# Retention and two MLPs: outputs and partial sums get buffers of their own, and three early steps are put in another order

## The chip, the core and the metric

The kernel runs on one core of one Trainium2 chip. The metric is the device time of one execution in microseconds (us); lower is better. The engines are named as in the profile: PE multiplies matrices (PEld loads its weights), DVE works on vectors, ACT applies functions and copies, POOL is the general engine, SP issues most of the transfers. Each engine takes its instructions in the order in which they are written in the program, and an instruction waits until what it reads has been written and what it overwrites has been read. L568 is line 568 of the kernel before.

## The reference

Four sequences of 768 tokens with 8 heads of width 64 go through a retention layer, and its output, as 3072 rows of 512, through two MLPs with 2048 hidden units each:

```python
for t in range(S):
    state = gamma * state + einsum('bhd,bhe->bhde', k[:, :, t], v[:, :, t])
    y[:, :, t] = scale * einsum('bhd,bhde->bhe', q[:, :, t], state)
x = y as (batch * seq, heads * head_dim)
h = x @ moe_w_in;   x = (h * cos(h)) @ moe_w_out
h = x @ moe2_w_in;  out = where(h >= 1, h, where(h <= -1, 0, (h + 1)**2 / 4)) @ moe2_w_out
```

All arrays are float32. Weights and activations are split into a high and a low part, and a product of 128 x 128 by 128 x 512 is made of three matmuls (high by high, low by high, high by low).

## The kernel before

**Chunks and blocks.** Retention is computed by chunks of 128 tokens. Chunk n is batch n % 4 at time n // 4, so the 24 chunks make 6 blocks of 4 chunks, 512 tokens each. For a chunk the kernel makes scores (`scores`, L475 for the first two blocks), masks them on DVE (`masks`, L522, or L528 and L541 later), and multiplies with values and with the state (`attend`, L597 and L604, later L585). `kv` (L557) makes a chunk's contribution to the state; `update` takes it out of PSUM: for chunks 0 to 3 it is a copy by ACT into `state` (L568), for chunks 4 to 7 two additions of `state` on DVE (L573), into a table `w` in one of five slots `w0` to `w4`. The slot that chunk 6's update takes, `w2`, held the decay table of the queries (`qdec`, read by `decay_q`, L463, on POOL, for chunks 4 to 7) and the keys of chunk 2. `finish_high` and `finish_low` split a chunk's output into the high part (ACT, L141) and the low part (DVE, L628) of the first MLP's input. `decay_k` (L453, POOL) scales the keys.

**Steps.** The first MLP is computed in 96 steps (k, b, j): k is the half of the hidden units (0 or 1), b the block, j one of 8 groups of 128 hidden units of that half. A step's first product (`first`, L687, 12 matmuls) makes 128 hidden units for 512 tokens in one PSUM bank; the phase is then rounded (`rounded`, ACT, L727), its fraction taken (`fraction`, DVE, L732), the cosine made (`cosine`, ACT, L738), the product h cos(h) formed (`product`, DVE, L741) and split (`high_part`, ACT, L745; `low`, DVE, L752). Three steps later the second product (`second`, L779, 12 matmuls) adds it to four banks, one for each 128 outputs of the block. Block 0 runs 5 steps, then block 1 its 8, then block 0 its last 3, then blocks 2 to 5; then the other half of the hidden units for blocks 0 to 5. The scores, attention and state work of later chunks lies between the products of the first 36 steps or so. Banks 4 and 5 take turns for the first product in the first 40 steps, banks 4 to 7 after that; banks 6 and 7 are the attention's in the first part, and one tile of both is shared by the scores, the output and the state contribution of a chunk. After the 96 steps the second MLP is computed (L991, L1007 and the lines around them).

**The order inside a step.** It is written by hand. `opening` writes it for steps 0 to 2, `act` for the others: rounding of this step, product and high part of the last step, fraction, `front`, low part of the last step, two outputs (`evacuate`), `mid`, cosine, two outputs, `fill`, `conv.advance`, `end`.

**Weights.** They come as pairs of 32-bit words (`raw`, L191, SP) and are converted in parts: `one` (two DVE instructions, L205 and L208), `two` (ACT, L215), `three` (DVE, L223), `four` (POOL, L232), `five` (ACT copy to the high part, L141) and `six` (POOL low part, L144). The first ten weights, called `w`, `w1`, `x[0]` to `x[2]` (of the first product) and `y[1]` to `y[5]` (of the second product), have their parts written out in the start and in the first steps; x[2] belongs to step 4. Later weights are converted by `conv.advance`.

**Outputs and sums.** When the last step of a block and a half has made its second product, `evacuate` takes the four banks out, each into a tile "o" of the ring "r" with 5 buffers, and SP stores it (L797). Phases of the steps are tiles of the same ring. For k = 0 the outputs are partial sums and go to DRAM (`yp`, and for block 0, which has two pieces, `yq`). For k = 1 `load_part` brings the partial sums back, into the tile of the block's own input `xt[1, b]`, once its last first product is through; L790 (DVE) adds them, into a tile of the ring "r", and SP stores it to `yT`. `load_parts` and `fetch_x` bring the input of the next block into the two buffers each of "xh" and "xl".

Of the kernel before, what the change touches and what calls it, by code (L numbers as in the profile page):

```python
# [11 lines left out]
F32 = mybir.dt.float32  # L12
F32R = mybir.dt.float32r
BF16 = mybir.dt.bfloat16
I32 = mybir.dt.int32
U32 = mybir.dt.uint32
AF = mybir.ActivationFunctionType
ALU = mybir.AluOpType
# [3 lines left out]
P = 128  # L22
C = 128
TB = 512
# [16 lines left out]
def tile_retention_mlp_mlp(  # L41
# [16 lines left out]
    nc = tc.nc  # L58
    NCH = qk.shape[0]
    T, DM = out.shape  # L60
    NF = w1.shape[0]
    NH = NF // 2
    NP = DM // P
    NC = kdec.shape[1]
    NB = T // TB
    D = 64
    CB = TB // C
    NEW = 2 * CB
    LAG = 3
# [9 lines left out]
    yp_d = [dram.tile([P, NP, TB], F32, name=f"yp{j}") for j in range(NB)]  # L79
    yq_d = dram.tile([P, NP, TB], F32, name="yq")  # L80
# [22 lines left out]
    wpool = [sbuf("wpool0", 1)]  # L103
# [71 lines left out]
    class Convert:  # L175
# [14 lines left out]
            src = (w1, w2)[self.m][self.j][:, self.a * TB:(self.a + 1) * TB]  # L190
            nc.sync.dma_start(out=self.raw.rearrange("p n w -> p (n w)"), in_=src.bitcast(I32))  # L191

        def one(self):
            if self.ready:
                self.f = spare_tile("f", self.few)
                nc.sync.dma_start(out=self.f, in_=w32_d[self.m, self.j, self.a])
                return
            n = 3 - self.late
            self.s = self.stage.tile([P, TB], I32, tag="cs", name="cs", bufs=n)
            if self.store:  # L200
                self.f = self.stage.tile([P, TB], F32, tag="cf", name="cf", bufs=n)
            else:
                self.f = spare_tile("f", self.few)
            f = self.f.bitcast(I32)
            nc.vector.tensor_scalar(  # L205
                out=self.f, in0=self.raw[:, :, 1].bitcast(F32), scalar1=2.0 ** -112, scalar2=None, op0=ALU.mult
            )
            nc.vector.tensor_scalar(  # L208
                out=f, in0=f, scalar1=3, scalar2=None, op0=ALU.logical_shift_left
            )  # L210

        def two(self):
            if self.ready:
# [132 lines left out]
    class Attention:  # L346


        def __init__(self, es):
            self.ap = es.enter_context(tc.tile_pool(name="att", bufs=1, reuse_waits="tile"))  # L350
            ac = es.enter_context(tc.tile_pool(name="attc", bufs=1))
            self.kdec_sb = ac.tile([P, NC, 2 * NP], F32, name="kdec_sb")
            self.state = [ac.tile([P, NP, D], F32, name=f"state{i}") for i in range(CB)]
            self.t, self.kd, self.v, self.qd = {}, {}, {}, {}
            self.kq, self.m, self.w = {}, {}, {}
            self.sc, self.pm, self.kvs, self.y = {}, {}, {}, {}
# [308 lines left out]
    def fetch_x():  # L665
        for t, d in coming[:3]:
            nc.sync.dma_start(out=t, in_=d)
        del coming[:3]

    def load_part(b, es, eng=nc.sync):  # L670

        for t, d in zip(xt[1, b], (yp_d[b], yq_d)[:1 + (b == 0)]):
            t = t.bitcast(F32)
            for e in es:
                eng.dma_start(out=t[:, e, :], in_=d[:, e, :])
                part.setdefault((b, e), []).append(t[:, e, :])
# [13 lines left out]
            )  # L690
        hs[k, b, j] = h

    def act(k, b, j, done=(), fill=(), mid=(), end=(), front=()):


        done = iter(done)
        now = Parts(k, b, j)
        now.rounded()
        last = parts.pop() if parts else None
        if last:  # L700
            last.high()
        now.fraction()
        for f in front:
            f()
        if last:
            last.low()
        evacuate(done, 2)
        for f in mid:
            f()
        now.cosine()  # L710
        evacuate(done, 2)
        for f in fill:
            f()
        conv.advance()
        for f in end:
            f()
        parts.append(now)
# [39 lines left out]
    def second(i, between=()):  # L757
# [24 lines left out]
            )  # L782
        return [(k, b, e, to) for e in range(NP)] if last else ()

    def evacuate(done, n):
        for k, b, e, to in itertools.islice(done, n):
            a, o = acc[k, b][e], tp.tile([P, TB], F32, tag="r", name="o", bufs=5)
            add = part.pop((b, e)) if k else []
            if add:
                nc.vector.tensor_tensor(out=o, in0=a, in1=add.pop(0), op=ALU.add)  # L790
            elif e % 2 == 0:
                nc.vector.tensor_copy(out=o, in_=a)
            else:
                nc.scalar.activation(out=o, in_=a, func=AF.Copy)
            for x in add:
                nc.gpsimd.tensor_tensor(out=o, in0=o, in1=x, op=ALU.add)
            nc.sync.dma_start(out=to[:, e, :], in_=o)  # L797
# [570 lines left out]
    def run():  # L1368
        i = 0
        with ExitStack() as es:  # L1370
            att = Attention(es)
            top.append(es.enter_context(tc.tile_pool(name="ps_att", bufs=1, space=PSUM, reuse_waits="tile")))
            stage = es.enter_context(tc.tile_pool(name="stage", bufs=1, reuse_waits="tile"))

# [41 lines left out]
            def scores(n):  # L1416
                att.scores(n, at[n])
                att.masks(n)
# [18 lines left out]
            w.three()  # L1437
            w.four()
            att.finish_low(0)
            att.finish_low(1)  # L1440
            scores(3)
            att.attend(2, single(at[2][0]))
            att.finish_high(2)
            w.five()
# [1 line left out]
            att.finish_low(2)  # L1446
            att.attend(3, single(at[3][0]))
            att.decay_k(0)
            w1.one()
            att.finish_high(3)  # L1450
            att.finish_low(3)
            w1.two()
            w1.three()
            w1.four()
# [7 lines left out]
            def opening(i, n):  # L1462


                now = Parts(*steps[i])
                if i == 0:
                    x[0].three()
                    now.rounded()
                    w1.five()
                    w1.six()  # L1470
                    now.fraction()
                    att.update(0)
                    att.decay_q(CB)
                    x[0].four()
                    att.masks(CB)
                    now.cosine()
                    att.decay_k(CB)
                elif i == 1:
                    now.rounded()
                    att.update(1)  # L1480
                    x[1].two()
                    now.fraction()
                    att.update(n)
                    att.decay_q(n + 1)
                    att.decay_k(n + 1)
                    att.decay_k(2)
                    att.decay_k(3)
                    att.masks(n + 1)
                    now.cosine()
                    x[1].three()  # L1490
                    x[1].four()
                    att.finish(n, now.product)
                else:
                    y[1].three()
                    now.rounded()
                    now.fraction()
                    att.update(n)
                    att.decay_q(n + 1)
                    y[1].four()
                    att.decay_k(n + 1)  # L1500
                    att.finish_high(n)
                    now.cosine()
                    att.masks(n + 1)
                    att.finish_low(n)
                    x[2].one()
                    y[1].five()
                    y[1].six()
                    for m in (2, 3):
                        att.update(m)
                    x[2].two()  # L1510
                    x[2].three()
                    x[2].four()
                if i != 1:
                    now.product()
                now.high_part()
                now.low()
                if i == 1:
                    y[1].one()
                    y[1].two()
                elif i:  # L1520
                    att.decay_q(n + 2)
                x[i].five()
                x[i].six()
                if i == 0:
                    x[1].one()
# [21 lines left out]
            for i in range(NH * (NB - 1)):  # L1547
# [16 lines left out]
                for n in decay if i >= LAG else ():  # L1564
                    att.decay_q(n)
                    att.decay_k(n)
                mid, end, fill, between, front = [], [], [], [], []
                for n in attend:
                    by, bk = place.get(i, (7, 6))
                    yb, kb = duo(by, bk)  # L1570
                    if NEW <= n < NEW + CB:
                        between.append(lambda n=n, yb=yb: att.attend(n, yb))
                        front.append(lambda n=n: att.finish_high(n))
                        mid.append(lambda n=n: att.finish_low(n))
                        continue
                    att.attend(n, yb)
                    att.kv(n, kb)
                    mid += [lambda n=n: att.finish(n), lambda n=n: att.update(n)]
                for n in early:
                    att.scores(n, (6, 7))  # L1580
# [13 lines left out]
                else:  # L1594
                    if i - 1 in y:
# [4 lines left out]
                        else:  # L1600
                            for f in (c.one, c.two, c.three, c.four):
                                f()
                            mid += [c.five, c.six]
                    act(*steps[i], done, fill, mid, end, front)
                    if i == LAG:
                        y[5].load(stage)
                send_x()
# [2 lines left out]
                elif i >= 2 * NH and i % NH == 2:  # L1610
                    store_parts(steps[i][1])
            i += 1
            assert not todo
            conv.slots = []
            conv.late = True
# [147 lines left out]
```

## Time and profile before

| | us |
|---|---|
| median of 3 runs | 1078.02 (1076.34 to 1080.09) |
| the profiled execution, its own time | 1080.16 |
| its span, first to last instruction | 1078.4 |
| PE busy | 1065.6 (99%) |
| DVE busy | 798.6 (74%) |
| ACT busy | 603.6 (56%) |
| POOL busy | 601.9 (56%) |

All views are of the profiled execution. A busy engine is one with an instruction in work; matmuls are pipelined, so that twelve that take 390 ns each follow each other every 227 ns, and are through in 2.72 us. "Idle before" is the time that an engine stood before an instruction, and the releaser is what ended it, inferred from the events of the semaphores: where several things were waited for, the one that came last by the records is named.

### The profile page before, as it was taken

The page shows a single profiled execution, that of the slowest core. Times are in us where ns is not written, and L with a number is a line of the kernel's source. Part 1 is how long each engine was busy: PE and PEld are TensorE (multiplying, and loading weights), DVE is VectorE, ACT ScalarE, POOL GpSimd, SP SyncE. Part 2 cuts the span into 40 slices and gives each one's busy share as a digit, 9 for nine tenths or more (in the row PEclk, how much of TensorE's full clock was granted, in tenths as well). Part 3 has the DMA queues.
Part 4 walks back from the last instruction along what each step waited for, and adds up shares of the span by engine and source line. Part 5 has one row for each costly group of instructions (what it writes and reads, how often), then busy time and mean ns, then how long its engine had stood idle before and what let it go on. Part 6 is the DMA issues. An engine that isn't in the chain of part 4 may idle for free.

```text
span 1078.4 us, 17871 instructions
## 1 busy us (share of the span) xinstructions
PE 1065.6 (99%) x6295; PEld 869.9 (81%) x6296; DVE 798.6 (74%) x1094; ACT 603.6 (56%) x1076; POOL 601.9 (56%) x515
## 2 busy tenths in 40 slices
PE   8999999999999999999999999999999999999998
PEld 5787787778888888888888888888888888888887
DVE  6977778786756547777874587778888777887875
ACT  3454333333355455555555666777668686675764
POOL 3845112221235457877997367796639886364560
PEclk9999999999999999999999999999999999999999
DMA  9579379896769579999898676989689889586642
GB/s 348 180 241 306 116 245 301 271 302 204 211 182 330 186 250 307 333 321 326 290 300 290 229 251 208 321 275 379 227 247 323 316 288 395 170 268 195 200 139 92
DMA packets 140137, 279.43 MB, mean 259 GB/s; under 512 B 15504, under 2 KB 42256, under 8 KB 140048
## 3 DMA queue, kind: packets, MB, share of 16 engines
q1 hardware_dynamic: 125072, 251.02, 70.4%
q10 hardware_dynamic: 14976, 27.27, 7.2%
q8 instruction: 50, 0.82, 0.3%
q14 instruction: 39, 0.32, 0.1%
HBM read 194.60 MB, written 83.62 MB: 258 GB/s over the span
## 4 chain that ended last, share of the span: by engine, by line
PE 91%; DVE 3%; DMA 3%; POOL 2%; issue 1%; ACT 0%; SPq 0%; DVEq 0%; POOLq 0%; ACTq 0%
PE b L779 24%; PE b L687 23%; PE b L991 20%; PE y L1007 19%; PE b L585 2%; DMA raw<-in_w 1%; PE b L1123 1%; PE b L492 1%; DVE big L1068 1%; DMA yp<-o 1%; PE b L503 1%; POOL cf L232 0%; POOL wil L144 0%; POOL kq L463 0%; DMA wo<-wp 0%
## 5 line engine op out<-in xcount | busy, mean ns | idle before, releaser
L727 ACT ACTIVATE r<-b 128x512 int32<-128x512 f32 x96 | 57.0, 594 | 185.4 <-PE b L687 123.3
L732 DVE SCALAR_TENSOR_TENSOR r<-b,r 128x512 f32<-128x512 f32 x96 | 65.9, 687 | 109.5 <-ACT r L727 105.1
L232 POOL TENSOR_TENSOR cf<-cf,cs 128x512 int32<-128x512 int32 x42 | 54.1, 1289 | 137.6 <-DVE cf L223 92.6
L1060 DVE TENSOR_TENSOR xh<-y,xh 128x1024 f32<-128x1024 f32 x86 | 105.0, 1221 | 30.6 <-PE y L1007 29.0
L779 PE MATMUL b<-gh,wo 128*128 128x512 f32 x384 | 98.4, 390 | 0.0
L1179 POOL TENSOR_TENSOR ft<-r,f 128x512 f32<-128x512 f32 x23 | 29.9, 1300 | 116.9 <-PE y L1007 86.7
L687 PE MATMUL b<-xh,wi 128*128 128x512 f32 x384 | 94.8, 389 | 0.0
L991 PE MATMUL b<-wih,wi 128*128 128x512 f32 x320 | 87.2, 390 | 0.4 <-DVE b L1171 0.4
L1060 DVE TENSOR_TENSOR xl<-y,xl 128x1024 f32<-128x1024 f32 x63 | 76.6, 1216 | 13.1 <-PE y L1007 13.1
L1007 PE MATMUL y<-gh,wo 128*128 128x512 f32 x276 | 85.0, 389 | 0.0
L779 PEld LDWEIGHTS b<-gh,wo 128*128 128x128 f32 x384 | 71.7, 188 | 16.0 <-DVE o L790 0.8
L687 PEld LDWEIGHTS b<-xh,wi 128*128 128x128 f32 x384 | 72.1, 188 | 15.0
L745 ACT ACTIVATE gh<-b 128x512 fp32r<-128x512 f32 x96 | 57.1, 595 | 43.1 <-DVE b L741 43.1
L687 PE MATMUL b<-xh,wih 128*128 128x512 f32 x192 | 76.0, 401 | 3.4 <-DVE gl L752 2.7
L779 PE MATMUL b<-gh,woh 128*128 128x512 f32 x192 | 77.3, 408 | 0.0
L687 PE MATMUL b<-xh,wil 128*128 128x512 f32 x192 | 75.0, 395 | 0.0
L779 PE MATMUL b<-gh,wol 128*128 128x512 f32 x192 | 74.0, 390 | 0.0
L991 PEld LDWEIGHTS b<-wih,wi 128*128 128x128 f32 x320 | 59.8, 188 | 13.8 <-DVE b L1171 1.3
L1007 PE MATMUL y<-wi,wo 128*128 128x512 f32 x276 | 70.0, 389 | 0.0
L1007 PE MATMUL y<-wo,wo 128*128 128x512 f32 x276 | 70.0, 389 | 0.0
L738 ACT ACTIVATE r<-r 128x512 f32<-128x512 f32 x96 | 60.6, 631 | 15.5 <-DVE r L732 15.4
L752 DVE TENSOR_TENSOR gl<-b,gh 128x512 fp32r<-128x512 f32 x96 | 65.6, 684 | 4.1 <-ACT gh L745 2.1
(174 smaller groups left out, 2789.3 us busy)
## 6 DMA issues: line engine op xcount, KB each, us to landing
wi<-wp SPq DMA_DIRECT2D x66, 512.0 KB, 4.7
raw<-in_w SPq DMA_DIRECT2D x64, 512.0 KB, 6.0
wo<-wp SPq DMA_DIRECT2D x63, 512.0 KB, 5.1
wp<-whi SPq DMA_DIRECT2D x48, 256.0 KB, 4.4
wp<-s SPq DMA_DIRECT2D x32, 256.0 KB, 4.7
w<-cf ACTq DMA_DIRECT2D x26, 256.0 KB, 5.3
xTh<-xh ACTq DMA_DIRECT2D x24, 256.0 KB, 5.6
xTl<-xl ACTq DMA_DIRECT2D x24, 256.0 KB, 5.7
```

Source lines behind the costliest of these rows:

```text
L232: nc.gpsimd.tensor_tensor(out=f, in0=f, in1=self.s, op=ALU.add)
L687: nc.tensor.matmul(out=h, lhsT=w[:, c * P:(c + 1) * P], rhs=x[:, c, :], start=(i == 0), stop=(i == len(terms) - 1),)
L727: nc.scalar.activation(out=self.r.bitcast(I32), in_=self.h, func=AF.Identity, scale=INV_2PI, bias=0.25)
L732: nc.vector.scalar_tensor_tensor(out=self.r, in0=self.h, scalar=INV_2PI, in1=self.r.bitcast(I32), op0=ALU.mult, op1=ALU.subtract,)
L738: nc.scalar.activation(out=self.r, in_=self.r, func=AF.Sin, scale=TWO_PI, bias=HALF_PI)
L745: nc.scalar.activation(out=self.gh, in_=self.h, func=AF.Copy)
L752: nc.vector.tensor_tensor(out=self.gl, in0=self.h, in1=self.gh.bitcast(F32), op=ALU.subtract)
L779: nc.tensor.matmul(out=acc[k, b][e], lhsT=w[:, s], rhs=g, start=(begin and i == 0), stop=(last and i == 2),)
L991: nc.tensor.matmul(out=to, lhsT=w[:, c * P:(c + 1) * P], rhs=x, start=begin and n == 0, stop=n == len(terms) - 1, skip_group_check=not begin,)
L1007: nc.tensor.matmul(out=to[:, e, :], lhsT=w[:, e * P:(e + 1) * P], rhs=a, start=begin and m == 0, stop=m == 2, skip_group_check=not begin,)
L1060: nc.vector.tensor_tensor(out=a, in0=y, in1=a, op=ALU.add)
L1179: nc.gpsimd.tensor_tensor(out=o, in0=x, in1=z, op=ALU.subtract)
```

## The change

- **Ring of outputs.** A new function `out_tile` gives the tile of an output. While the attention runs, outputs 0 and 1 of a block go to a ring "o" of two buffers in the attention's pool, outputs 2 and 3 to the ring "r" as before. Outputs of block 4's first half go to the tiles of weights 15 that are not loaded yet, those of block 5's first half to tiles of weights that are used up.
- **Partial sums.** `load_part` takes new tiles "xh" (for block 0 also "xl") of the two buffers, in place of views of `xt[1, b]`; `evacuate` adds in place, into the partial sum's tile, for blocks 0 to 4 of the second half.
- **States.** The four tiles `state` move into the low-part tiles of the weights of j = 7.
- **Start.** `scores(3)`, with its masks, goes ahead of `finish_low(1)`; `w1.one` is cut in two with `finish_low(3)` between.
- **Step 2.** The copies of the states of chunks 2 and 3 go ahead of x[2].one, y[1].five and y[1].six. Product, high part and low part of step 2, and x[2].five and x[2].six, leave `opening`; the product, the high and the low part are then done in step 3 by `act`, as in all later steps.
- **Step 3.** A new list `pre` holds `finish_high`, `update` and `finish_low` of chunk 6, x[2].five and x[2].six. `act` runs the first ahead of the last step's product and the others behind it, ahead of the fraction.

```diff
-        def one(self):
+        def one(self, *which):
+            if which == (1,):
+                f = self.f.bitcast(I32)
+                nc.vector.tensor_scalar(
+                    out=f, in0=f, scalar1=3, scalar2=None, op0=ALU.logical_shift_left
+                )
+                return
...
-            self.state = [ac.tile([P, NP, D], F32, name=f"state{i}") for i in range(CB)]
+            at = [wpool[0].tile([P, TB], F32, tag=f"w{t}l{NH - 1}", name="state") for t in "io"]
+            at = [t[:, o:o + TB // 2] for t in at for o in (0, TB // 2)]
+            self.state = [t.rearrange("p (c e) -> p c e", c=NP) for t in at]
...
     def load_part(b, es, eng=nc.sync):
-        for t, d in zip(xt[1, b], (yp_d[b], yq_d)[:1 + (b == 0)]):
-            t = t.bitcast(F32)
+        ds = (yp_d[b], yq_d)[:1 + (b == 0)]
+        if b not in halves:
+            halves[b] = [xpool.tile([P, NP, TB], F32, tag=t, name="yp") for t, _ in zip(("xh", "xl"), ds)]
+        for t, d in zip(halves[b], ds):
...
-    def act(k, b, j, done=(), fill=(), mid=(), end=(), front=()):
+    def act(k, b, j, done=(), fill=(), mid=(), end=(), front=(), pre=()):
         done = iter(done)
         now = Parts(k, b, j)
         now.rounded()
         last = parts.pop() if parts else None
+        for f in pre[:1]:
+            f()
         if last:
             last.high()
+        for f in pre[1:]:
+            f()
         now.fraction()
...
+    own = []
+
+    def out_tile(k, b, e):
+        if own and callable(own[0]) and e < 2:
+            return own[0]("o", TB, 2)
+        if (k, b) == (0, NB - 2):
+            if e % 2 == 0:
+                nm = ("wi", "wo")[e // 2]
+                own.append(wpool[1].tile([P, 2, TB], F32, tag=f"{nm}{NF - 1}", name="o"))
+            return own[-1][:, e % 2, :] if e % 2 == 0 else own.pop()[:, 1, :]
+        if (k, b) == (0, NB - 1):
+            return wpool[0].tile([P, TB], F32, tag=f"woh{e}", name="o")
+        return tp.tile([P, TB], F32, tag="r", name="o", bufs=5)
+
     def evacuate(done, n):
         for k, b, e, to in itertools.islice(done, n):
-            a, o = acc[k, b][e], tp.tile([P, TB], F32, tag="r", name="o", bufs=5)
-            add = part.pop((b, e)) if k else []
+            a, add = acc[k, b][e], part.pop((b, e)) if k else []
+            o = add[0] if k and b < NB - 1 else out_tile(k, b, e)
...
             att = Attention(es)
+            own.append(att.ring)
...
             att.finish_low(0)
+            scores(3)
             att.finish_low(1)
-            scores(3)
...
-            w1.one()
             att.finish_high(3)
+            w1.one(0)
             att.finish_low(3)
+            w1.one(1)
...
                     att.finish_low(n)
+                    for m in (2, 3):
+                        att.update(m)
                     x[2].one()
                     y[1].five()
                     y[1].six()
-                    for m in (2, 3):
-                        att.update(m)
                     x[2].two()
                     x[2].three()
                     x[2].four()
-                if i != 1:
+                if i == 2:
+                    att.decay_q(n + 2)
+                    parts.append(now)
+                    return
+                if i == 0:
                     now.product()
...
                     att.attend(n, yb)
                     att.kv(n, kb)
+                    if i == LAG:
+                        pre = [
+                            lambda n=n: att.finish_high(n), lambda n=n: att.update(n),
+                            lambda n=n: att.finish_low(n), x[2].five, x[2].six,
+                        ]
+                        continue
                     mid += [lambda n=n: att.finish(n), lambda n=n: att.update(n)]
...
             i += 1
+            own.clear()
```

## Rows read from the trace of the kernel before

**Rows 1.** The page, first part: busy us (share of the span) x instructions.
```profile
PE 1065.6 (99%) x6295; PEld 869.9 (81%) x6296; DVE 798.6 (74%) x1094; ACT 603.6 (56%) x1076; POOL 601.9 (56%) x515
```

**Rows 2.** PE's waits: waiting line, releaser: us in total, times, longest.
```profile
PE b L687 <- DVE gl L752: 2.7, 2, 2.0
```

**Rows 3.** The chain that ended last, in order: start us, us, what.
```profile
5.03 12.82 DMA raw<-in_w
...
51.16 4.54 PE b L687 x12
...
61.20 2.72 PE b L687 x12
...
89.05 3.01 PE b L687 x12
...
216.57 3.02 PE b L687 x12
...
578.27 3.28 PE b L779 x12
```

**Rows 4.** Timeline of PE: start us, us, instruction [idle before <-releaser].
```profile
42.83 1.09 PE L597 MATMUL b<-kq,state 64*64 64x128 f32 x16 [0.80 <-POOL kd L453]
...
50.00 1.16 PE L475 MATMUL b<-qk 64*128 64x128 f32 x16 [1.64 <-issue]
```

**Rows 5.** Timeline of ACT, at three places.
```profile
40.02 0.63 ACT L738 ACTIVATE r<-r 128x512 f32<-128x512 f32 x1 [1.55 <-DVE r L732]
...
42.37 0.64 ACT L568 ACTIVATE state<-b 128x256 f32<-128x256 f32 x2
...
87.07 0.60 ACT L727 ACTIVATE r<-b 128x512 int32<-128x512 f32 x1 [3.73 <-DMA yp<-o]
...
214.60 0.60 ACT L727 ACTIVATE r<-b 128x512 int32<-128x512 f32 x1 [5.54 <-PE b L779]
```

**Rows 6.** Timeline of DVE: masks and update of step 3's surroundings, step 27's product.
```profile
41.38 0.68 DVE L522 TENSOR_TENSOR w<-b,dtab 128x512 f32<-128x512 f32 x1
...
49.05 0.85 DVE L573 TENSOR_TENSOR w<-b,state 64x256 f32<-64x256 f32 x2
...
52.27 0.68 DVE L522 TENSOR_TENSOR w<-b,dtab 128x512 f32<-128x512 f32 x1
...
211.75 0.69 DVE L741 TENSOR_TENSOR b<-b,r 128x512 f32<-128x512 f32 x1
```

**Rows 7.** Timeline of POOL around step 3.
```profile
46.62 1.29 POOL L463 TENSOR_TENSOR kq<-qk,w 128x512 f32<-128x512 f32 x1
47.87 1.29 POOL L144 TENSOR_TENSOR wil<-cf,wih 128x512 fp32r<-128x512 f32 x1
49.10 1.05 POOL L453 TENSOR_TENSOR kd<-kd,kdec_sb 128x512 f32<-128x512 f32 x1
```

**Rows 8.** Windows: us, busy us by engine (instructions), PE's granted clock, DMA share, GB/s.
```profile
48.00:50.00 2.00, 0.36 (x3) 0.04 (x1) 1.96 (x5) 1.38 (x3) 2.00 (x2) 1.00 0.02 8
...
52.00:54.00 2.00, 2.00 (x6) 1.52 (x5) 1.93 (x5) 0.91 (x2) 1.26 (x2) 0.50 0.53 143
...
215.00:220.00 5.00, 3.43 (x44) 2.66 (x48) 4.07 (x8) 2.68 (x6) 0.00 (x0) 1.00 0.94 271
```

**Rows 9.** ACT's waits from 320 to 600 us.
```profile
ACT r L727 <- DMA yT<-o: 22.3, 3, 8.8
```

**Rows 10.** Instructions of the tile o: ns min/median/max, and landing of its stores.
```profile
L790 DVE TENSOR_TENSOR o<-b,xh x24: 677/680/691, 400.5 to 622.2; 128x512 f32<-128x512 f32 x24
...
DMA to landing us min/median/max: 2.0/3.4/9.0
```

**Rows 11.** Timeline of SP's queue at the first block's end in the second half.
```profile
402.64 4.07 SPq L797 DMA_DIRECT2D yT<-o  x4
406.77 0.42 SPq L196 DMA_DIRECT2D f<-w  x1
407.28 0.41 SPq L667 DMA_DIRECT2D xh<-xTh  x1
```

**Rows 12.** DVE's waits over the whole span.
```profile
DVE qk L528 <- DMA mtab<-in_tabs: 1.9, 1, 1.9
```

More of the change, by code (lines that the diff above doesn't have):

```diff
@@ L203, in one @@
                 self.f = spare_tile("f", self.few)
-            f = self.f.bitcast(I32)
             nc.vector.tensor_scalar(
@@ L207, in one @@
             )
-            nc.vector.tensor_scalar(
-                out=f, in0=f, scalar1=3, scalar2=None, op0=ALU.logical_shift_left
-            )
+            if not which:
+                self.one(1)
         def two(self):
@@ L668, in fetch_x @@
         del coming[:3]
+    halves = {}
     def load_part(b, es, eng=nc.sync):
-        for t, d in zip(xt[1, b], (yp_d[b], yq_d)[:1 + (b == 0)]):
-            t = t.bitcast(F32)
+        ds = (yp_d[b], yq_d)[:1 + (b == 0)]
+        if b not in halves:
+            halves[b] = [xpool.tile([P, NP, TB], F32, tag=t, name="yp") for t, _ in zip(("xh", "xl"), ds)]
+        for t, d in zip(halves[b], ds):
             for e in es:
@@ L1519, in opening @@
                     y[1].two()
-                elif i:
-                    att.decay_q(n + 2)
                 x[i].five()
@@ L1566, in run @@
                     att.decay_k(n)
-                mid, end, fill, between, front = [], [], [], [], []
+                mid, end, fill, between, front, pre = [], [], [], [], [], []
                 for n in attend:
@@ L1603, in run @@
                             mid += [c.five, c.six]
-                    act(*steps[i], done, fill, mid, end, front)
+                    act(*steps[i], done, fill, mid, end, front, pre)
                     if i == LAG:
```

## The prediction

> **What bounds the kernel now.** The page's first part comes first: PE is busy 1065.6 us of a span of 1078.4 [rows 1]. Some 12 us at most can come from PE's waits, so an edit is worth only what it takes from a wait that PE itself feels. The list of PE's waits has at its head L752, an instruction of DVE: 2.7 us in two waits, the longer of 2.0 [rows 2]. The chain of work, in order of time, then gives places and full prices, because a group of 12 matmuls takes 2.72 us there when nothing is late [rows 3]. The groups of steps 10 and 28 are the two behind L752: they start at 89.05 and 216.57, and take 3.01 and 3.02 us besides, as PE has to fill again. Before each, the ACT rounding (L727) of the step before had waited long, and with it DVE's fraction and L752 [rows 5]. The third group out of line is step 4's first product, 4.54 us from 51.16. PE's timeline shows what stands ahead of it: chunk 6's attention (L597) starts at 42.83 after 0.80 idle, the scores of chunk 7 (L475) at 50.00 after 1.64 idle [rows 4]. From 227 us on nearly every group stands at 2.72 us; nothing there can give more than tenths.
>
> **The change, part by part.** The sum is made against the profiled execution's own 1080.16 us (span 1078.4 and 1.8 around it), which is 2.14 above 1078.02, the median of the three runs.
>
> *Outputs leave the ring of five.* Before, the four outputs of a block and the phases in work share the five buffers "r". At 87.07 the rounding had stood 3.73 us, put down to the store yp<-o; at 214.60 it had stood 5.54 us, put down to PE's L779 [rows 5]. The rounding reads the first product, which by then was long done, and needs nothing else but a buffer, so I take the second for the same wait. A store lands 2.0 to 9.0 us after its issue [rows 10]. With the change two of four outputs go to a ring of their own while the attention runs; two outputs and two phases leave one of five free, and no rounding waits for a store. On PE this is worth, for step 10, 0.65 idle (2.7 less 2.0) and 3.01 - 2.72 of filling, **0.94 us**; for step 28, 2.0 and 3.02 - 2.72, **2.3 us** [rows 2, 3]. Next late would be DVE: its product before that rounding's fraction starts at 211.75 and takes 0.6, then fraction and L752 as much each, through by 213.7, ahead of PE, which was ready at 216.57 - 2.0 = 214.57 [rows 3, 6]. In the second half of the program the roundings stand 22.3 us on the store yT<-o [rows 9], and PE's groups are at 2.72 all the same; so that counts as nothing. What covers it is that four banks take turns for the first product there; without them it would be up to 8.8 us a time. The sum in place is the same DVE instruction of 0.68 us [rows 10], and as many transfers are issued as before.
>
> *States sooner.* L597 of chunk 6 reads the state that ACT copies from 42.37 on (L568), behind the copy of a weight that needs POOL [rows 5]. The row of L597 blames POOL's kd, which ended at that moment, but L597 does not read kd. Moved ahead of the weight, the two copies (0.64) follow the cosine, which ends at 40.65, and are done by 41.3. Next late is chunk 6's mask, whose banks L597 takes over: the second of the pair, 41.38 + 0.68 = 42.06 [rows 6]. So L597 starts at 42.1, 0.7 us sooner.
>
> *Chunk 6 finished ahead of the phase.* Scores of chunk 7 need banks 6 and 7, which hold chunk 6's output and update; the update is read last, on DVE, until 49.05 + 0.85 = 49.90, and L475 starts at 50.00 [rows 4, 6]. The edit puts update (L573) and L628 of chunk 6 ahead of step 3's fraction. But this update writes a slot whose old tile also holds the queries' decay table, and the last to read that is POOL's L463 of chunk 7, until 46.62 + 1.29 = 47.91 [rows 7]. What POOL does before it stays, and DVE gives it its input no sooner. So DVE, after step 2's delayed product (to about 45.8), stands some 2.1 us; then update to 48.76, L628 to 49.36, and L475 at about 49.5. PE, through with the second product at 50.00 - 1.64 - 0.7 = 47.66, idles 1.8 us. Of both edits **0.5 us** is left.
>
> Queued on DVE behind the standing update: step 3's fraction, step 2's low part (its product and high part now come in this phase too), a weight conversion of 1.7 us, and chunk 7's masks, done at 53.5 rather than 52.95 [rows 6]. PE reads the masks after step 4's first product and the low part in step 5. On POOL, chunk 7's kd now comes ahead of step 4's wil: 47.91 + 1.05 + 1.29 = 50.25 [rows 7]; its reader is the second matmul of the product that starts at 49.5 + 1.1 = 50.6. Free, with a third of a microsecond to spare. The ACT copies in front (rounding, high parts of chunk 6 and step 2, a weight) end at 47.3 and wait for none of this.
>
> *The clock.* The group of 4.54 us ran at half the clock: granted 0.50 from 52 to 54 us (1.2 GHz), after two microseconds in which PE was busy for 0.36 [rows 8]. But after the 2.0 us idle before 216.57 the stretch from 215 to 220 kept 1.00 [rows 8]. Two rows, two outcomes. The new idle of 1.8 us is a little longer than the old 1.64 and stands between the same matmuls, so I take the nearer row: the clock falls again, and the gain stays 0.5. If it doesn't, step 4's product ends at 50.6 + 2.72 = 53.3, the masks let the attention start at 53.6 instead of 51.16 + 4.54 = 55.7, and the gain is 2.1. These are the bounds, 0.5 and 2.1.
> The Trainium skill (TensorE: Matmul & The Clock Gate, section What's actually happening) holds that the slow level is the default, and that only recent activity holds the clock up. By that rule a longer idle stretch speaks for another fall, against this change, and the gain would be the lower bound. The row of 52 to 54 agrees with it; the row of 215 to 220 does not show it.
>
> *Order at the start.* Chunk 3's masks go ahead of chunk 1's L628, and chunk 3's L628 between the halves of a conversion. PE's first product may start some 0.6 us sooner. But the chain there doesn't run through PE: raw weights land at 5.03 + 12.82 = 17.85 [rows 3], then come DVE's three conversions and that one L628, as many in either order, and POOL's queue. Counted as nothing; between 0 and 0.6.
>
> *State tiles in weights' places, partial sums in tiles of their own.* Same instructions; those weights are made steps after the states' last reader. Loads of the block after next now wait until the sum's store has left the tile. On SP they followed the four stores at once, at 407.28 [rows 11]; now they, and all behind them, wait 2.0 to 9.0 us more [rows 10], at four block ends. Cover: weights are loaded one or two steps (5.4 to 10.9 us) before use. Taken as nothing; the bound is a rival.
>
> Sum: 0.94 + 2.3 + 0.5 = 3.7 us. An execution like the profiled one would take 1080.16 - 3.7 = 1076.4; against the median it is 1074.3.
>
> **The rivals.**
> (a) *The clock stays up:* 0.94 + 2.3 + 2.1 = 5.3, so 1072.7. For it stands the row at 215, against it the row at 52.
> (b) *The update doesn't wait for the decay table:* L475 at 47.7, step 4's product held by wil at 50.25 and through at 52.8, the attention 2.9 sooner, the clock up; 6.1 in all, 1071.9. Against it: slot and order in the code.
> (c) *A stall is given back later:* at step 24 DVE already waits 1.9 us for a table of the masks [rows 12]; PE ahead by 2 to 3 us may meet a table or weights that come no sooner. A loss the size of the smaller stall or the larger, 0.94 to 2.3, leaves 1.4 to 2.8: 1075.2 to 1076.6.
> (d) *Slower:* the loads that wait on SP hold up weight transfers behind them, DVE waits for these in its queue, and sums at a block's end free PE's banks late. A late sum cost 3.28 - 2.72 = 0.56 at 578.27 [rows 3]. It decides when each of four block ends costs PE over 3.7 / 4 = 0.93; with stores of 9.0 us less one step of 5.44 it is 3.6 each, 14 in all, 1088. Against it: the same stage hid the roundings' 22.3 us.
> (e) *It doesn't do what it says:* the rounding at 214.60 waited for something else; 1.4 is left, 1076.6.
>
> **How the numbers follow.** Forecast 0.42, (a) 0.24, (b) 0.05, (c) 0.15, (d) 0.07, (e) 0.07. The runs of before spread 3.7 us, so 0.3% (3.2 us: below 1074.8 or above 1081.3) is about what can be told from no change. The forecast lies half a microsecond under that bound, and some 0.27 of its 0.42 counts as faster: 0.27 + 0.24 + 0.05 = 0.56. Slower is (d), 0.07; the rest is 0.37. The range goes from (b) to the upper end of (c) and (e), 0.3 wider on each side for a median's own spread: 1071.6 to 1076.9. Outside are (d) and a tenth of chance.
>
> **What would show it.** Right: no rounding stands on a store before 230 us, and steps 10 and 28 follow without a gap; L568's copies end before 41.5, and L597 starts near 42.1; DVE stands some 2 us ahead of chunk 6's update, until POOL's L463 is done; L475 near 49.5. The granted clock from 51 to 55 us decides between forecast and (a). Wrong: a new wait of PE on a table between 90 and 300 us, or groups over 2.8 us at the block ends of the second half.

## The result: slower, by what was counted as nothing

| | median, us | runs | ratio to before, 95% interval |
|---|---|---|---|
| before | 1078.97 (1076.27 to 1082.03) | 8 | |
| after | 1084.12 (1082.37 to 1089.75) | 8 | 1.0054 [1.0031, 1.0077] |

The forecast was 1074.3, the range 1071.6 to 1076.9. The kernel is 5.8 us slower by that ratio, which is one of means, and 5.2 between the medians; the forecast had it 3.7 faster. The profiled execution of after took 1084.71, span 1082.9. Lines stand a little lower in the kernel after: L697 is the first product, L793 the second, L741 the rounding, L818 the sum in place, L673 the loads of x, L825 the stores of outputs.

The page of after, first part, answers to [rows 1], and the list of PE's waits, in part, to [rows 2]:

```profile
PE 1067.9 (99%) x6295; PEld 870.4 (80%) x6296; DVE 794.4 (73%) x1094; ACT 604.6 (56%) x1076; POOL 601.8 (56%) x515
```
```profile
PE b L697 <- DMA xh<-xTh: 3.4, 2, 3.2
...
PE b L793 <- ACT o L822: 0.6, 1, 0.6
...
PE b L793 <- DVE yp L818: 0.3, 1, 0.3
PE b L697 <- DVE gl L766: 0.3, 1, 0.3
```

The two waits behind DVE's gl, 2.7 us, are down to 0.3. At the head stands a wait that the list of before did not have: for a piece of the block's input x, 3.2 us. The chain of work, start and length, shows where:

```profile
49.94 3.01 PE b L697 x12
...
85.61 2.91 PE b L697 x12
...
219.13 3.03 PE b L697 x12
...
466.88 7.89 DMA xh<-xTh
...
474.81 2.93 PE b L697 x6
477.74 4.32 PE b L793 x12
```

Step 4's product, 4.54 us in [rows 3], takes 3.01. The rows at 85.61 and 219.13 are steps 10 and 29; PE starts step 29's product 4.3 us ahead of before (219.13 for 223.47). At 474 the gain is lost. The next views are PE's timeline of after, the same place of before, and two windows of after (busy time by engine, then the granted clock):

```profile
470.10 1.52 PE L697 MATMUL b<-xh,wi 128*128 128x512 f32 x6
474.81 1.22 PE L697 MATMUL b<-xh,wi 128*128 128x512 f32 x2 [3.19 <-DMA xh<-xTh]
475.83 1.91 PE L697 MATMUL b<-xl,wi 128*128 128x512 f32 x4
```
```profile
471.95 1.98 PE L687 MATMUL b<-xh,wi 128*128 128x512 f32 x8
```
```profile
472.00:474.00 2.00, 0.00 (x0) 0.00 (x0) 0.81 (x2) 0.00 (x0) 1.92 (x4) 1.00 0.91 280
...
476.00:478.00 2.00, 2.00 (x7) 1.52 (x6) 0.14 (x1) 0.22 (x1) 1.25 (x1) 0.50 1.05 404
```

The first six matmuls of a block run, the seventh stands 3.19 us for the block's last piece, and what follows runs at half the clock (0.50). PE's start of the same product goes from 1.9 ahead of before (470.10 for 471.95) to 4.5 behind (487.34 for 482.83): 6.4 us, half idle, half slow clock.

SP's queue tells why the piece is late. After, then before:

```profile
450.67 2.19 SPq L825 DMA_DIRECT2D yT<-yp  x4
455.70 0.32 SPq L673 DMA_DIRECT2D xh<-xTh  x1
...
466.88 0.39 SPq L673 DMA_DIRECT2D xh<-xTh  x1
```
```profile
451.70 2.00 SPq L797 DMA_DIRECT2D yT<-o  x4
453.75 0.64 SPq L667 DMA_DIRECT2D xh<-xTh  x1
...
464.95 0.32 SPq L667 DMA_DIRECT2D xh<-xTh  x1
```

In before SP asks for x right behind the stores (451.70 + 2.00 = 453.70). In after it stands 2.84 us (452.86 to 455.70), until the last of the stores, which read the tile that x is to take, has landed (455.59); the last pair is asked for 16.2 us after the first store, not 13.25. In before the last high piece lands at 464.95 + 7.34 = 472.29 and the seventh matmul is due at 471.95 + 6 x 0.227 = 473.31: 1.02 to spare. In after it lands at 466.88 + 7.89 = 474.77 and is due at 470.10 + 1.36 = 471.46: 2.48 later, PE 1.85 sooner, 3.3 short. (The expectations below reckon with 0.94 and 2.4, from a landing put 0.08 too late.) It is not much in any execution: the two others of before (before_again and before_third, below) have 0.39 and 0.26 to spare here, and all three have 0.1 to 0.6 at the start of the last block (555 to 559 us). SP's waits show the stand eight times, 1.9 to 4.1 us at each of four block ends:

```profile
SPq L673 <- DMA yT<-yp: 11.6, 8, 4.0
```

### The profile page after: what moved, and what is told of

Read it like the earlier page. It is cut to its first block, busy times and chain, and to the rows that moved or that the text cites. A ratio compares the mean times of both kernels' runs of the same rounds, so it can differ in the third digit from the quotient of the medians.

```text
span 1082.9 us, 17823 instructions
## 1 busy us (share of the span) xinstructions
PE 1067.9 (99%) x6295; PEld 870.4 (80%) x6296; DVE 794.4 (73%) x1094; ACT 604.6 (56%) x1076; POOL 601.8 (56%) x515
## 4 chain that ended last, share of the span: by engine, by line
PE 71%; DMA 12%; DVE 8%; POOL 3%; issue 2%; ACT 2%; SPq 1%; ACTq 0%; DVEq 0%; POOLq 0%
PE b L1019 20%; PE y L1035 18%; PE b L793 14%; PE b L697 14%; DMA raw<-in_w 3%; DMA xh<-xTh 1%; DMA wo<-w 1%; PE b L591 1%; PE b L1151 1%; DMA wp<-f 1%; DMA wp<-whi 1%; DVE big L1096 1%; DMA w<-cf 1%; DMA dtab<-in_tabs 1%; DVE cf L227 1%
## 5 line engine op out<-in xcount | busy, mean ns | idle before, releaser
L741 ACT ACTIVATE r<-b 128x512 int32<-128x512 f32 x96 | 57.2, 595 | 176.9 <-PE b L697 148.2
L793 PE MATMUL b<-gh,wo 128*128 128x512 f32 x384 | 100.0, 395 | 1.0 <-ACT o L822 0.6
L697 PE MATMUL b<-xh,wi 128*128 128x512 f32 x384 | 96.2, 391 | 3.5 <-DMA xh<-xTh 3.4
L697 PEld LDWEIGHTS b<-xh,wi 128*128 128x128 f32 x384 | 72.1, 188 | 19.5 <-DMA xh<-xTh 4.8
L793 PEld LDWEIGHTS b<-gh,wo 128*128 128x128 f32 x384 | 72.8, 191 | 17.7 <-ACT o L822 1.0
L697 PE MATMUL b<-xh,wih 128*128 128x512 f32 x192 | 75.4, 398 | 2.1 <-ACT xh L141 1.4
L793 PE MATMUL b<-gh,woh 128*128 128x512 f32 x192 | 77.3, 407 | 0.0
L697 PE MATMUL b<-xh,wil 128*128 128x512 f32 x192 | 74.0, 391 | 0.1
L793 PE MATMUL b<-gh,wol 128*128 128x512 f32 x192 | 74.0, 390 | 0.0
```

Source lines behind the costliest of these rows:

```text
L697: nc.tensor.matmul(out=h, lhsT=w[:, c * P:(c + 1) * P], rhs=x[:, c, :], start=(i == 0), stop=(i == len(terms) - 1),)
L741: nc.scalar.activation(out=self.r.bitcast(I32), in_=self.h, func=AF.Identity, scale=INV_2PI, bias=0.25)
L793: nc.tensor.matmul(out=acc[k, b][e], lhsT=w[:, s], rhs=g, start=(begin and i == 0), stop=(last and i == 2),)
```

## The theories

**A**: the sum kept in the partial sum's tile makes SP stand on the sum's store; what lies behind (x, weights) comes late. **B**: x comes at SP's own pace, and PE, ahead by the gains of the front, ran into it. **C**: the partial sums' loads into tiles of their own are in the way. And for the gains, since before's profiled execution lay 2.1 above the median: **D**, the losses that were priced at steps 4 and 28 belonged to that execution; **E**, they belong to the kernel.

## The experiments

**sum_in_ring.** After, the sums of the second half in the ring again:

```diff
-            o = add[0] if k and b < NB - 1 else out_tile(k, b, e)
+            o = out_tile(k, b, e)
```

> The kernel after, but the sums of the second half go to the ring r again; partial sums keep their own tiles. Theory A (the sum's store holds its tile, SP stands on it, the last piece of x comes 2.4 us later than before and PE, 1.85 us ahead, waits 3.2 for it and then runs slow): no wait of SP on yT<-yp, the wait at 475 us shrinks from 3.2 to about 0.9, the clock stays up, 5.5 less than after: about 1078.6. Theory B (the pieces come at the pace of the weights on SP whatever the sums do, and PE only ran ahead of them): the wait and the slow stretch stay, about 1084. Theory C (the partial sums' loads into tiles of their own are in the way): about 1084.

Measured: 1078.25 us (12 runs), ratio 0.9996 [0.9981, 1.0011], as A had it. No wait of SP on the stores is left:

```profile
447.18 2.01 SPq L825 DMA_DIRECT2D yT<-o  x4
449.29 0.59 SPq L673 DMA_DIRECT2D xh<-xTh  x1
...
460.80 0.32 SPq L673 DMA_DIRECT2D xh<-xTh  x1
```

The last pair comes 13.6 us after the first store, as in before, and PE waits nowhere between 360 and 550. One line gives back the whole loss. C falls, since the partial sums kept their tiles here.

**before_sum_tile.** Before, with partial sums in their own tiles and the sum in place, and nothing else of the change:

```diff
+    halves = {}
...
-        for t, d in zip(xt[1, b], (yp_d[b], yq_d)[:1 + (b == 0)]):
-            t = t.bitcast(F32)
+        ds = (yp_d[b], yq_d)[:1 + (b == 0)]
+        if b not in halves:
+            halves[b] = [xpool.tile([P, NP, TB], F32, tag=t, name="yp") for t, _ in zip(("xh", "xl"), ds)]
+        for t, d in zip(halves[b], ds):
...
+            o = add[0] if k and b < NB - 1 else tp.tile([P, TB], F32, tag="r", name="o", bufs=5)
```

> The kernel before with one part of the change alone: partial sums in tiles of their own and the sum in place. Theory A: SP stands on yT<-yp at the block ends; the last piece of x comes 2.4 later at 475 us, where there was 0.94 to spare, so PE waits 1.5 there: 1080.5, and up to 1082 if the clock falls. Theory B: without the lead no wait: 1079. Theory C: 1081 to 1084, with the loss at the partial sums' loads.

Measured: 1084.17 us (6 runs), 1.0055 [1.0034, 1.0076]: 5.9 us slower, as much as the whole change and more than expected. PE's waits and SP's:

```profile
PE b L691 <- DMA xh<-xTh: 3.8, 3, 1.9
...
PE b L783 <- ACT cs L215: 0.9, 1, 0.9
```
```profile
SPq L667 <- DMA yT<-yp: 12.0, 8, 3.7
```

There are three waits for x, at 472 and 560, and one of 0.9 at 444 us, where the second product needs a bank that a late sum on DVE still holds. (The row names a weight copy on ACT, which the product doesn't read; the first of four sums starts at 443.14, the product at 443.96.)

**early_only.** After, with that part undone: the edit of sum_in_ring, and `load_part` as in before.

> The kernel after without that part: partial sums in the views of the input tile and sums in the ring r as before; the ring of outputs, the states and the early steps as changed. Theory A: the front's 4.0 us stay gained but for some 2 that PE's lead gives back to weights in the second half, and a wait of 0.9 for x: 1076 to 1078. Theory B: the lead alone brings the wait and the slow clock, 1080 to 1084. Theory C: 1075.

Measured: 1078.29 us (12 runs), 1.0002 [0.9987, 1.0017]. In its trace PE is 4.1 us ahead of before's at 444 and still at 550, with no wait for x: the lead alone does not make the loss, so B falls as its cause. Tenths it can cost: ring_only (below), as far ahead and with the sums in the ring, waits 0.2 us for x at 469 and 0.6 at 557, and its time shows no loss. But A's number was missed too, if by little: the rest of the change brings no measurable gain.

**x_four and x_four_again.** After, with x asked for sooner; the second is another execution of the same kernel:

```diff
-        for t, d in coming[:3]:
+        for t, d in coming[:4]:
...
-        del coming[:3]
+        del coming[:4]
```

> The kernel after, but the eight pieces of a block's x are asked for by fours in two steps, not by threes in three; the last two pieces come a step (5.4 us) sooner. Theories A and B: no wait of PE for x at 475 and 565 us, the 6.35 us lost at 475 come back: about 1077.5. Theory C: no change, about 1084. If the earlier requests hold up the weights behind them on SP, a new wait shows at another place.

Measured: 1084.48 us (1079.2 to 1087.94, 7 runs), 1.005 [1.0027, 1.0074]. A miss: as slow as after. Its profiled execution, 1079.35, was one of the two fastest and has no wait at 475, so it did not show the typical loss.

> The kernel after with x asked for by fours, a second profiled execution; its other runs lay 5 us above the first profiled one. Theory A2 (SP's stand on the sums' stores also makes raw weights late behind it, so that DVE's sums in place come late and PE waits for banks at a block's end): the x pieces are in time at 475 us, but PE waits for a sum or a weight at one of the block ends, 1 to 2 us and again as much by the clock. Rival: PE waits for x all the same.

Measured: 1081.13. PE's timeline, then DVE's, and DVE's at the same place of early_only, whose sums are in the ring:

```profile
445.99 2.43 PE L793 MATMUL b<-gh,wo 128*128 128x512 f32 x8 [2.62 <-DVE yp L818]
```
```profile
436.63 0.82 DVE L210 TENSOR_SCALAR f<-raw 128x512 f32<-128x512 f32 x1 [4.64 <-DMA raw<-in_w]
...
445.16 2.47 DVE L818 TENSOR_TENSOR yp<-b,yp 128x512 f32<-128x512 f32 x4
```
```profile
432.75 0.76 DVE L210 TENSOR_SCALAR f<-raw 128x512 f32<-128x512 f32 x1 [2.75 <-DMA raw<-in_w]
```

No wait for x at 475; in its place PE stands 2.62 us at 446 for a sum, behind DVE, which had stood 4.64 for a raw weight (2.75 in early_only) and ran late from there. SP asked for that weight 32.1 us after the first store of the block end before it (430.48 for 398.38); in after it is 30.5, in early_only 27.3. So sooner requests for x mend only x; weights behind SP's stand are late as well. The trace of x_four has the same wait at 444, 1.2 us long. What the slower executions of this kernel lost was not recorded, so how the 5 us came about in them stays open.

**x_later_four.** After with the sum still in place; x by fours, and in the second half a step later, when the stores have had time to land:

```diff
-                if n < len(blocks) and l == LAG - 1:
+                if n < len(blocks) and l == (LAG - 1, LAG)[blocks[n][0] and blocks[n][1] > 1]:
```

> The kernel after with the sums still in place, but the x loads that come to lie behind their stores are asked for one step (5.4 us) later and by fours, so that the stores have landed when SP comes to them and the last pieces are asked for no later than in after. Theory A (it is SP's stand on the stores, 11.6 us in eight waits, that costs): no wait of SP on yT<-yp over 0.5, and 1078 to 1079.5. Rival F (the sum in place costs by itself, or the x pieces have too little time anyway): 1083 to 1086.

Measured: 1079.65 us (12 runs), 1.0003 [0.999, 1.0017]. Two of SP's eight waits are left, not none:

```profile
SPq L673 <- DMA yT<-yp: 4.6, 2, 3.1
```

They are at 452 and 494; 7 of the 11.6 us are gone. So with the sums still in place the loss is gone as well (-1.1 to +1.8 us against before): F falls, the rival in which the sum in place costs by itself.

**before_x_late.** Before, with that later request alone, still by threes.

> The kernel before, but x is asked for one step (5.4 us) later in the second half; sums as before. Theory A holds that a block's last pieces of x have far less than a step to spare (0.94 us at 472 us): PE waits some 4.5 us at the start of each of the last blocks, 14 to 18 us in all, and more where the clock falls. If the pieces had a step or two of cover, as the prediction took for weights, no wait shows.

Measured: 1085.79, with one wait:

```profile
PE b L687 <- DMA xh<-xTh: 6.7, 1, 6.7
```

It stands at 433 us, the start of block 2's second half; with the slow clock behind it PE lost 8.5. A miss: a step less was too much at one block start, not at four. At the later ones PE was 8.5 us later too, so what they bear with PE on time stays open.

**before_again, before_third, after_again.** The two kernels unchanged, other executions.

> The kernel before, unchanged, a second execution with a profile. Theory D (the idle of 2.0 at step 28 and the half clock at step 4 belonged to the execution that was read, not to the kernel): at most one of the two shows; the first product of step 28 starts 2 to 4 us sooner than 216.57 us. Rival E (they belong to the kernel): both show again, at 51 and 216.6 us within 0.5. The 0.65 idle at step 10, behind a rounding that stands on a store, shows again by both.

> The kernel before, unchanged, a third execution with a profile. As for the second: theory D gives at most one of the two losses, of 1.7 at step 4 and 2.3 at step 28; rival E gives both.

> The kernel after, unchanged, a second execution with a profile. Theory A: SP stands eight times on yT<-yp, 10 to 12 us in all; between 440 and 570 us PE waits for x or for a sum, 4 to 7 us lost in all, with or without the half clock that made 3.2 of the 6.35 at 475 us the first time. No stall at step 10.

Measured: 1079.05, 1075.54 and 1084.35. The waits of PE that [rows 2] had at 2.7 in two, in the second and in the third execution of before:

```profile
PE b L687 <- DVE gl L752: 0.8, 1, 0.8
```
```profile
PE b L687 <- DVE gl L752: 0.2, 1, 0.2
```

Neither has a stall at step 28 or a slow clock at step 4: D holds. After_again repeats the loss at 473, with the clock at 0.50 behind it:

```profile
PE b L697 <- DMA xh<-xTh: 2.8, 1, 2.8
```

**ring_only and steps_only.** Before with `out_tile`, its ring and the states' new places alone; before with the order of the start and of steps 2 and 3 alone.

> The kernel before with the ring of outputs (and the states and outputs in weights' places) alone. If the ring takes away the stall of step 10 and nothing else: no idle before the first product of step 10 (0.65 to 0.82 in three of four traces of before), 0.9 us less, 1077.5; what it may win at step 28 is not in every execution, so no more than that. Rival: the store was not what the rounding stood on, the idle stays, 1078.4.

> The kernel before with the other order of the start and of steps 2 and 3 alone. The forecast's 0.5 at step 4: from PE's first product to the first product of step 4 some 0.2 to 0.5 us less than in traces of before, the stall of step 10 as before, 1078.0. Rival: the order gains nothing that lasts, 1078.4.

Measured: 1078.84 us (12 runs), 1.0004 [0.999, 1.0018], and 1078.32 (12 runs), 0.9995 [0.9981, 1.0009]. Neither part moves the time by what can be told. The 14 traces together say what each gives, from PE's timelines (us of idle before the first product; "slow" where the clock fell in or around step 4's product):

| front | idle at step 10 | idle at step 28 | slow at step 4 |
|---|---|---|---|
| old ring, old steps (5 traces) | 0.65, 0.82, 0.20, 0.82, 0 | 2.01, 0, 0, 0, 0 | 1 of 5 |
| old ring, new steps (steps_only) | 0 | 0 | 1 of 1 |
| new ring, old steps (ring_only) | 0 | 0 | 0 of 1 |
| both new (7 traces) | 0 in all | 0 in all | 3 of 7 |

And how far ahead (-) or behind PE is at the same product, against before's profiled execution:

| at, us of before | 72 | 94.6 | 223.5 | 336 | 445 | 488 | 598 |
|---|---|---|---|---|---|---|---|
| before_again | -1.8 | -1.6 | -3.0 | -1.5 | -1.7 | -1.7 | -2.1 |
| before_third | -2.5 | -2.9 | -5.6 | -4.5 | -4.3 | -4.3 | -4.7 |
| before_sum_tile | -1.7 | -1.5 | -4.4 | -4.4 | -4.5 | -0.8 | +1.0 |
| ring_only | -1.2 | -2.1 | -4.4 | -4.1 | -4.3 | -3.8 | -3.5 |
| early_only | -2.2 | -3.1 | -4.7 | -4.3 | -4.1 | -4.1 | -3.9 |
| sum_in_ring | -0.2 | -1.1 | -3.4 | -2.5 | -2.5 | -2.5 | -2.8 |
| after | -2.8 | -3.5 | -4.3 | -4.0 | -2.8 | +4.5 | +4.4 |
| after_again | -0.9 | -1.4 | -3.4 | -2.9 | -3.0 | +2.9 | +2.3 |

Before itself wanders by 5.6 us up to 224, with nothing changed. Between 445 and 598 the three traces of the table in which SP stands on all the stores lose 5.5 (before_sum_tile), 7.2 (after) and 5.3 us (after_again); the others lose 0.8 at most.

## Why the prediction was wrong

**The step that failed** is "State tiles in weights' places, partial sums in tiles of their own": "Taken as nothing". It measured 5.9 us (before_sum_tile), and taking the sum out of the tile gives them back (sum_in_ring). The wait was seen (2.0 to 9.0 at each of four block ends; it is 1.9 to 4.1 in after, and 10.9 to 12.0 in eight waits in every trace that has all of them), but its cover was reckoned for the wrong transfer: weights, used one or two steps later. The first thing behind SP's stand is x itself, whose last piece had 1.02 us to spare. The prediction's sign of being wrong came where x was late: six matmuls in 2.93 us and a group of 4.32 from 474.81 on. Rival (d) had the right mechanism, with a chance of 0.07; its 14 us were over twice too much, since one or two block starts pay, not four, and its path, weights late and then a sum late, was the smaller one in the traces of after and before_sum_tile (waits of 0.3 to 0.9 us) and the larger only where x came sooner (x_four_again).

**Step 28, 2.3 us.** The mechanism could not be seen again: the stall stands in one of six traces with the old ring, though the rounding stood on a store in others too (3.02 before 211.41 in before_again). The step took a stall of one execution for one of the kernel. That this execution lay 2.14 above the median was written down, and the same gain was then taken from the median.

**Step 10, 0.94 us.** Right in kind: idle in four of the six traces with the old ring, in none of the eight with the new one. In the mean over the six it is 0.4, not 0.65. In after, as forecast, no rounding before 230 us is put down to a store of outputs.

**States and chunk 6, 0.5 us.** The chain of waits came as told, and 0.8 us sooner than told (chunk 6's attention starts at 41.29, not 42.1), as PE's first product did. In after, DVE, then PE:

```profile
47.03 0.86 DVE L579 TENSOR_TENSOR w<-b,state 64x256 f32<-64x256 f32 x2 [2.11 <-POOL kq L469]
```
```profile
48.70 1.16 PE L481 MATMUL b<-qk 64*128 64x128 f32 x16 [1.89 <-issue]
```

The update stood 2.1 us for the decay table, as predicted, and PE stood 1.89, where 1.8 was predicted. The scores, 1.3 sooner than in before (48.70 for 50.00), came 0.5 sooner by the steps alone. From the first product to that of step 4, six traces with the old order take 32.5 in the mean, eight with the new one 32.5: the 0.5 is not there in the mean. The slow clock stands in four of the eight, behind the longer idle, and in one of the six with the old; so few traces don't show whether the longer idle brings it.

**The clock.** "The nearer row: the clock falls again" held in half of the executions, and not in the one profiled. The Trainium skill (TensorE: Matmul & The Clock Gate, section What's actually happening) says that the clock's monitor is free-running and does not reset when a kernel starts, so that the point of a change varies; by that, one kernel may fare either way. These traces agree in that: behind 1.89 us of idle at step 4 after kept the full clock (1.00 from 50 to 52 us) and steps_only did not (0.50). The reason they don't show.

**Order at the start**, counted as nothing: the first product starts at 18.03 us in the mean of the eight traces with the new order (17.61 to 18.65), at 18.40 in the mean of the six with the old (18.20 to 18.61). Some 0.4, within the bounds of 0 to 0.6.

**In sum** the front may be worth about 1 us (an estimate: 0.4 of idle and some filling at step 10, 0.4 at the start), which 12 runs can't tell from nothing (early_only: -1.4 to +1.8 us). None of the versions tried beats before.

## What to carry to other kernels

When an operation is made to work in place, ask who reuses its tile: the next load now waits for the store's landing, not for the arithmetic, and it waits in the issuing queue with everything behind it. Reckon the cover for each transfer behind that wait, beginning with the one that has least to spare, by the time of its first reader less its landing. And before a stall is priced, look whether a second execution has it: a profile that lies above the median holds losses that no edit will give back.

## What the runs showed of the hardware

The clock's fall after an idle stretch of PE was not a matter of the stretch alone. At step 4 the same 1.63 to 1.65 us of idle ended in half clock in one trace of six, 1.84 to 1.89 in four of eight. Later, 1.91 us at 472 (before_sum_tile) kept the full clock, as this window shows, and so did 2.62 us at 446 (x_four_again, 1.00 from 444 to 452), while 2.84 and 3.19 us (after_again, after) and 6.75 us (before_x_late) did not:

```profile
472.00:476.00 4.00, 3.65 (x16) 3.04 (x17) 3.93 (x6) 2.48 (x4) 2.74 (x3) 1.00 1.04 396
```

A fall doubled the price of a wait: 3.19 us of idle cost 6.4 in after, 2.84 cost 6.0 in after_again (PE from 3.0 ahead to 2.9 behind).

A transfer's wait is paid in the queue that issues it. The Trainium skill (DMA: Bandwidth & Descriptors, section Anatomy of one DMA — SWDGE (gpsimd) path) says that the DMA engines wait on no semaphore, the issuing sequencer does before it dispatches; that section is on transfers that POOL issues, but SP's eight waits agree (11.6 us in after). The delay runs through the queue: the first piece of x was asked for 1.95 us later than in before (455.70 for 453.75), the last pair, 11 us on, still 1.93 later.
